# Four head pairs of the third batch transposed by DMA, the loads behind them held, and two edits in the first batch

## The chip, the cores and the metric

The kernel runs on one core of one Trainium2 chip. A core has TensorE (PE, with its weight loads as PEld), VectorE (DVE), ScalarE (ACT), GpSimd (POOL) and SyncE (SP), and 16 DMA engines that all queues share. The metric is the device time of one execution in microseconds; lower is better. Before the change three runs took 434.40 to 435.32 us, with a median of 434.78.

## The reference

There are 8 batches of 12 heads, with 448 positions and a head width of 64. Attention comes without a softmax, and behind it a gated feed-forward layer with 1536 inner columns:

```python
scores = scale * q @ k.T                # per batch and head, scale = 1/8
attn   = maximum(scores, 0) ** 2 / 448
x      = (attn @ v), heads side by side # 3584 x 768
out    = (maximum(x @ w_gate, 0) * (x @ w_val)) @ w_out
```

Inputs and output are float32. The kernel works in bfloat16 with float32 sums.

## The kernel before

All matmuls go through `mm` (L64). The heads are taken in six pairs per batch, and two pairs make a quad. For a score matmul both keys and queries must lie with the head width on the partitions, while they are loaded with positions on the partitions (`load_nat`, L109, two DMAs on POOL's queue: one for 64 partitions with four positions each, one for 64 partitions with three; the queue also turns float32 into bfloat16). So each pair has to be transposed, and there are two ways:

- On PE (batches 0, 1 and 2): `transposes` (L168) makes 16 small PE transposes into a PSUM tile `kq_ps`, and one DVE copy (L179) of 960 columns brings keys and queries to SBUF as `kq_sb`. 64 of the copied columns, between keys and queries, are not used.
- By DMA (batches 3 to 7, `PE_B = 3`): `dma_transposes` (L146) regroups all heads of the batch with one DVE copy for keys and one for queries (L151, into `kr` and `qr`), and SP issues four DMA transposes for each (L154), into `kT` and `qT`. The fourth of four has 64 rows, the others 128. There is one `kr` and one `qr`; `kT` and `qT` exist twice, by even and odd batches. `operands` (L157) gives the scores the one or the other.

**Order of the work.** Each engine runs its instructions in program order; the order is written out by hand. `batch(b)` (L436) takes 24 tiles in eight steps of three: six score tiles of pairs, a shared last tile and one "av" entry per quad (`tiles_later`, L351). A score tile goes through ACT's relu (L184) and DVE's square (L188) to `attn`; the values of a quad are cast by DVE (L458) to `xT`. Step n = 2 holds the last tile of the first quad, its "av", and the first score tile of pair 2. Between the steps stand "gaps", in which the feed-forward units of the batch before are run: twelve gate-and-value units (`gv_unit`, L257: twelve gate matmuls, ACT's relu L265, twelve value matmuls, DVE's product L271), then output units (`out_unit`, L283), whose results ACT copies (L294) and SP writes out (L302) from three `o_sb` buffers. `PAIRS_AT` (L434) says after which step which pair is transposed: pairs 2, 3, 4 and 5 in steps 0, 1, 3 and 4, and pairs 0 and 1 of the next batch in step 7. These transposes are put in `midway`, which runs between a unit's gate and value matmuls, or in the middle of an output unit. In the batches from b = 2 on, `dma_transposes(b + 1)` is called in step n = 2.

**Loads.** Keys, queries and values of batch b + 1 are issued in step 0 of batch b, all on POOL's queue. POOL runs ahead of the other engines: an issue waits only until its buffer (two per tensor, by even and odd batches) is free, or until the eighth DMA before it on this queue has landed. At the start (L333 to L344) the first four heads' keys come by SP and ACT; POOL loads queries 0 to 3, keys 4 to 7, queries 4 to 7, keys 8 to 11, queries 8 to 11, then values, the gate and value weights in four pieces, batch 1, and `load_wo` (the output weights in two halves).

**The first batch** (`first_batch`, L378) has no units to fill PE. It runs 21 score tiles, with `idle_matmuls` between them, and ends with six value computations in PSUM (`values`, `av_pair`), which `cast` brings to `xT`: four on DVE (L392) and two on ACT (L390). The names `u2`, `w0` and `w1` are score tiles; `relu2` issues a tile's relu on ACT and its square on DVE.

Of the kernel before, what the change touches and what calls it, by code (L numbers as in the profile page):

```python
# [10 lines left out]
BF16 = mybir.dt.bfloat16  # L11
# [5 lines left out]
def kernel(  # L17
# [15 lines left out]
    nc = tc.nc  # L33

    B, H, S, D = q.shape
    d_model, d_ff = moe_w_gate.shape
# [3 lines left out]
    HP = H // 2  # L40
# [9 lines left out]
    const = ctx.enter_context(tc.tile_pool(name="const", bufs=1))  # L50
    xpool = ctx.enter_context(tc.tile_pool(name="xpool", bufs=2))
    kqpool = ctx.enter_context(tc.tile_pool(name="kqpool", bufs=3))
# [7 lines left out]
    def pin(ins):  # L60
        return tc.keep_in_program_order(ins)
# [10 lines left out]
    NB = 2  # L72
# [4 lines left out]
    kn_b = [const.tile([128, H, 4, D], BF16, name=f"kn{i}") for i in range(NB)]  # L77
    qn_b = [const.tile([128, H, 4, D], BF16, name=f"qn{i}") for i in range(NB)]
# [11 lines left out]
    def make_ident():  # L90
        pin(nc.gpsimd.affine_select(out=ident, in_=ident, compare_op=ALU.not_equal, fill=1.0, base=0,  # L91
                                    pattern=[[-1, 128]], channel_multiplier=1))

    def dma_in(o, i):
        pin(nc.gpsimd.dma_start(out=o, in_=i))  # L95
# [13 lines left out]
    def load_nat(dst, src, b, h0, h1):  # L109
        lo = src[b, h0:h1, 0:256, :].rearrange("h (j i) d -> j h i d", i=4)  # L110
        hi = src[b, h0:h1, 256:448, :].rearrange("h (j i) d -> j h i d", i=3)
        dma_in(dst[0:64, h0:h1, :, :], lo)
        dma_in(dst[64:128, h0:h1, 0:3, :], hi)

    def load_qk(b, h0=0, h1=H):
        load_nat(kn_b[b % NB], k, b, h0, h1)
        load_nat(qn_b[b % NB], q, b, h0, h1)

    def load_v(b):
        load_nat(v_b[b % NB], v, b, 0, H)  # L120
# [19 lines left out]
            dma_in(wo_sb[c], rows.rearrange("(kf p) m -> p kf m", p=128))  # L140


    PE_B = 3
    kT_b = [const.tile([128, HP, 512], BF16, name=f"kT{i}") for i in range(NB)]
    qT_b = [const.tile([128, HP, 512], BF16, name=f"qT{i}") for i in range(NB)]
    def dma_transposes(b):  # L146

        n = b % NB
        for nat, grp, tr in ((kn_b[n], kr, kT_b[n]), (qn_b[n], qr, qT_b[n])):
            o = grp.rearrange("p i (h d) -> p i h d", d=D)  # L150
            pin(nc.vector.tensor_copy(o, nat.rearrange("p h i d -> p i h d")))  # L151
            for i in range(4):
                r = 128 if i < 3 else 64
                pin(nc.sync.dma_start_transpose(out=tr[:, :, i * 128:i * 128 + r], in_=grp[0:r, i, :]))  # L154


    def operands(b, hp, bank=None):  # L157

        if b >= PE_B:
            n = b % NB  # L160
            return kT_b[n][:, hp, 0:S], qT_b[n][:, hp, 0:S]
        kq = transposes(b, hp, bank)
        return kq[:, 0:S], kq[:, 512:512 + S]

    def sc_tile():
        return psum.tile([128, 2, 512], FP32, name="sc_ps", tag="sc", bufs=3)
# [1 line left out]
    def transposes(b, hp, bank):  # L168
        if bank is None:
            ps = psum.tile([128, 2048], BF16, name="kq_ps", tag="sc", bufs=3)  # L170
        else:
            ps = bank.bitcast(BF16)
        for t, c0 in ((kn_b[b % NB], 0), (qn_b[b % NB], 512)):
            for i in range(4):
                for h2 in range(2):
                    o = ps[h2 * 64:h2 * 64 + 64, c0 + i * 128:c0 + i * 128 + 128]
                    pin(nc.tensor.transpose(o, t[:, 2 * hp + h2, i, :], ident))  # L177
        kq = kqpool.tile([128, 512 + S], BF16, name="kq_sb")
        pin(nc.vector.tensor_copy(kq, ps[:, 0:512 + S]))  # L179
        return kq  # L180

    def relu_part(src, n):
        r = rpool.tile([128, 2, S], BF16, name="r_sb")[:, :n, :]
        pin(nc.scalar.activation(r, src, AF.Relu))  # L184
        return r

    def square_part(dst, r):
        pin(nc.vector.tensor_tensor(dst, r, r, ALU.mult))  # L188

    def relu2(src, dst, n):  # L190
        square_part(dst, relu_part(src, n))
# [40 lines left out]
    def bank_tile():  # L232
        return psum.tile([128, 512], FP32, name="xT_ps", tag="acc", bufs=2)
# [18 lines left out]
    def flush():  # L252
        flush_relu()
        while late_squares:
            square_part(*late_squares.pop(0))
# [69 lines left out]
    def gap():  # L325

        n, of, i = share
        for _ in range((i + 1) * n // of - i * n // of):
            ffn.pop(0)()
        flush()  # L330
        share[2] = i + 1

    load_first(4)  # L333
    make_ident()
    load_qk(0, 4, 8)
    load_qk(0, 8, H)
    load_v(0)
    load_gv(0)
    load_gv(1)
# [22 lines left out]
    def burst(b, tiles):  # L362

        todo, begun = [], None
        for qd, kind, c, i in tiles:
            attn = attn_of(b, qd)
            if kind == "pair":
                todo.append(scores(kqs[b, 2 * qd + c], i, attn, 8 * c + 2 * i))
            elif kind == "last":
                todo.append(scores_last((kqs[b, 2 * qd], kqs[b, 2 * qd + 1]), attn))  # L370
            else:
                ps = sc_tile()
                banks = [ps[:, c, :S] for c in range(2)]
                av_last(b, qd, attn, banks)
                begun = (qd, banks, ps[:, :, :S])
        return todo, begun

    def first_batch():  # L378

        def tile_of(n, i):  # L380
            return burst(0, [tiles_first[3 * n + i]])[0][0]

        def values(qd, c):
            ps, x = bank_tile(), xT_of[0][:, 2 * qd + c, :]
            av_pair(0, qd, c, attn_of(0, qd), ps)
            return x, ps[:, :S]

        def cast(x, ps, on_act=False):
            if on_act:
                pin(nc.scalar.activation(x, ps, AF.Copy))  # L390
            else:
                pin(nc.vector.tensor_copy(x, ps))  # L392

        bank = bank_tile()
        idle_matmuls(bank, 14)
        transpose_pair(0, 0, bank)
        bank = bank_tile()
        idle_matmuls(bank, 4)
        for n in range(5):
            t = [tile_of(n, i) for i in range(3)]  # L400
            if n == 4:
                low_values(0)
            transpose_pair(0, n + 1, bank)
            if n < 4:
                bank = bank_tile()
                idle_matmuls(bank, 2)
                for u in t:
                    relu2(*u)
        relu2(*t[0])
        relu2(*t[1])  # L410
        u0 = tile_of(5, 0)
        cast(*values(0, 0))
        relu2(*t[2])
        u1 = tile_of(5, 1)
        cast(*values(0, 1))
        u2 = tile_of(5, 2)
        relu2(*u0)
        relu2(*u1)
        w0 = tile_of(6, 0)
        cast(*values(1, 0), on_act=True)  # L420
        relu2(*u2)
        w1 = tile_of(6, 1)
        cast(*values(1, 1))
        w2 = tile_of(6, 2)
        relu2(*w0)
        relu2(*w1)
        x, ps = values(2, 0)
        relu2(*w2)
        cast(x, ps, on_act=True)
        cast(*values(2, 1))  # L430
# [5 lines left out]
    def batch(b):  # L436

        gaps = [(1, 1)] * 8
        if b == 1:
            gaps = [(0, 1), (0, 1), (0, 1), (0, 1), (0, 1), (0, 1), (1, 1), (1, 1)]  # L440
        elif b == 2:
            gaps[5] = (0, 2)
        start_gaps(sum(map(sum, gaps)))
        for n in range(len(tiles_later) // 3):
            todo, begun = burst(b, tiles_later[3 * n:3 * n + 3])
            relu2(*todo[0])
            relu2(*todo[1])
            late.extend(todo[2:])
            if n == 1:
                low_values(b)  # L450
            if n == 0 and b < B - 1:
                load_qk(b + 1)
                load_v(b + 1)

            def values():
                qd, banks, both = begun
                av_rest(b, qd, attn_of(b, qd), banks)
                pin(nc.vector.tensor_copy(xT_of[b][:, 2 * qd:2 * qd + 2, :], both))  # L458

            for _ in range(gaps[n][0]):  # L460
                gap()
            for hp in PAIRS_AT.get(n, ()):
                if hp < HP:
                    midway.append(lambda hp=hp: transpose_pair(b, hp))
                elif b + 1 < B:
                    midway.append(lambda hp=hp: transpose_pair(b + 1, hp - HP))
            if begun and (b, n) == (1, 2):
                midway.append(values)
            elif begun:
                values()  # L470
            if b + 1 < B and n == 2 and b + 1 >= PE_B:
                dma_transposes(b + 1)
            for _ in range(gaps[n][1]):
                gap()

    for b in range(B):
        xT_of[b] = xpool.tile([128, KD, S], BF16, name="xT")
# [46 lines left out]
```

## Time and profile before

| | |
|---|---|
| median of three runs | 434.78 us |
| the profiled execution | 435.1 us |
| its span, first to last instruction | 433.3 us |
| PE busy | 425.4 us |
| DVE, ACT busy | 210.7 us, 218.0 us |
| POOL busy | 49.0 us |
| granted PE clock | 1.0 throughout |
| moved by DMA | 42.45 MB |

In the profile each line of a timeline gives the start and the length in us, the engine, the line of the kernel, the operation, output and inputs, their shapes and the count; in brackets stands the idle time of the engine ahead of it and what ended it. "SPq" marks an instruction of SP's queue, such as a DMA issue: its length is that of the issue, and "to landing" counts from the issue's start until the data has arrived. A DMA share over 1 means that packets overlap on the engines. Lengths of matmuls on PE overlap by the pipeline, so what a stretch costs PE is read from the distance between starts.

### The profile page before, as it was taken

To read this page: it belongs to the slowest core of one execution; us is meant where nothing else is said; L and a number is where in the kernel's file an instruction comes from. 1 tells how busy PE (TensorE), PEld (TensorE's weight loads), DVE (VectorE), ACT (ScalarE), POOL (GpSimd) and SP (SyncE) were. 2 spreads that over 40 slices of the span, in tenths; PEclk is the share of its full clock that TensorE was granted. 3 is DMA by queue.
4 is the path that set the end of the run, shared out by engine and by line. 5 is a ranking of instruction groups with operands and counts; after the bars stand their busy time and mean duration, and the time that the engine had idled before them with its cause. 6 is when DMAs were issued, how large, how long until landed. Compare 5 with 4: busy or idle time off the path is not lost.

```text
span 433.3 us, 11436 instructions
## 1 busy us (share of the span) xinstructions
PE 425.4 (98%) x5068; PEld 250.3 (58%) x5068; DVE 210.7 (49%) x334; ACT 218.0 (50%) x325; POOL 49.0 (11%) x71
## 2 busy tenths in 40 slices
PE   8899999999999999999999999999999999999996
PEld 4457655655565555655566555655566555566564
DVE  5952784556623655356532565435643454422210
ACT  4942666454554564465454645554545645532221
POOL 8424311100204000300004000010000000000001
PEclk9999999999999999999999999999999999999999
DMA  9999999905679770591517932170414100030014
GB/s 151 181 205 195 203 205 211 204 5 81 106 145 166 103 112 19 104 198 34 97 38 128 176 66 65 38 138 2 101 29 106 42 2 2 12 100 2 2 38 109
DMA packets 78513, 42.45 MB, mean 98 GB/s; under 512 B 48352, under 2 KB 74976, under 8 KB 78464
## 3 DMA queue, kind: packets, MB, share of 16 engines
q0 software_dynamic: 45120, 23.47, 40.6%
q1 hardware_dynamic: 32992, 18.01, 17.8%
q8 instruction: 39, 0.64, 0.6%
q10 hardware_dynamic: 352, 0.25, 0.2%
q14 instruction: 10, 0.08, 0.1%
HBM read 47.19 MB, written 11.01 MB: 134 GB/s over the span
## 4 chain that ended last, share of the span: by engine, by line
PE 84%; DMA 12%; POOL 2%; issue 1%; POOLq 0%; ACT 0%
PE o_ps L64 25%; PE g_ps L64 23%; PE v_ps L64 22%; PE sc_ps L64 13%; DMA qn<-in_q_dram 5%; DMA wo<-in_moe_w_out_dram 5%; DMA vn<-in_v_dram 2%; POOL qn L95 1%; PE kq_ps L177 1%; POOL kn L95 1%; POOL vn L95 0%; POOL out_dram L302 0%; POOLq L519 0%; ACT o_sb L294 0%; POOL ident L91 0%
## 5 line engine op out<-in xcount | busy, mean ns | idle before, releaser
L184 ACT ACTIVATE r_sb<-sc_ps 128x896 bf16<-128x896 f32 x168 | 145.1, 927 | 39.4 <-PE sc_ps L64 39.4
L188 DVE TENSOR_TENSOR attn<-r_sb 128x896 bf16<-128x896 bf16 x168 | 103.7, 623 | 92.2 <-ACT r_sb L184 92.1
L64 PE MATMUL g_ps<-xT,wg 128*64 128x448 bf16 x1152 | 126.1, 354 | 0.0
L64 PE MATMUL v_ps<-xT,wv 128*64 128x448 bf16 x1152 | 125.2, 352 | 0.0
L64 PE MATMUL o_ps<-wo,hT 128*64 128x384 bf16 (+1 forms) x1368 | 115.3, 324 | 0.3 <-DMA wo<-in_moe_w_out_dram 0.3
L271 DVE TENSOR_TENSOR hT<-v_ps,g_sb 128x448 bf16<-128x448 f32 x96 | 59.9, 624 | 88.4 <-PE v_ps L64 87.5
L64 PEld LDWEIGHTS <-hT 128*64 128x64 bf16 x1368 | 75.5, 110 | 37.8 <-issue 6.5
L265 ACT ACTIVATE g_sb<-g_ps 128x448 bf16<-128x448 f32 x96 | 52.3, 545 | 88.9 <-PE g_ps L64 88.9
L64 PEld LDWEIGHTS <-wg 128*64 128x64 bf16 x1152 | 63.4, 110 | 49.8 <-issue 13.1
L64 PEld LDWEIGHTS <-wv 128*64 128x64 bf16 x1152 | 66.2, 110 | 41.0
L294 ACT ACTIVATE o_sb<-o_ps 128x384 f32<-128x384 f32 (+1 forms) x57 | 27.9, 489 | 81.4 <-PE o_ps L64 81.4
L64 PE MATMUL sc_ps<-attn,vn 128*64 128x448 bf16 (+1 forms) x336 | 35.1, 354 | 0.0
L95 POOL DMA_DIRECT2D vn<-in_v_dram x16 | 12.1, 768 | 168.5 <-PE sc_ps L64 161.0
L458 DVE CAST xT<-sc_ps 128x896 bf16<-128x896 f32 x21 | 22.9, 1091 | 14.3 <-PE sc_ps L64 14.3
L64 PEld LDWEIGHTS <-vn 128*64 128x64 bf16 (+1 forms) x384 | 18.8, 109 | 16.5 <-issue 5.6
L64 PE MATMUL sc_ps<-qT,kT 64*64 64x448 bf16 x420 | 28.4, 357 | 0.0
L64 PE MATMUL sc_ps<-kq_sb 64*64 64x448 bf16 x252 | 19.0, 360 | 1.9 <-ACT r_sb L184 1.7
L95 POOL DMA_DIRECT2D kn<-in_k_dram x18 | 13.3, 762 | 46.8 <-PE kq_ps L177 45.2
L64 PEld LDWEIGHTS <-kT 64*64 64x64 bf16 x420 | 9.6, 105 | 14.3 <-issue 11.7
L302 POOL DMA_DIRECT2D out_dram<-o_sb x2 | 1.1, 558 | 146.2 <-ACT o_sb L294 146.2
L95 POOL DMA_DIRECT2D qn<-in_q_dram x20 | 14.6, 752 | 9.4 <-DMA vn<-in_v_dram 6.3
L64 PEld LDWEIGHTS <-kq_sb 64*64 64x64 bf16 x252 | 6.5, 105 | 13.3 <-issue 9.9
(32 smaller groups left out, 84.2 us busy)
## 6 DMA issues: line engine op xcount, KB each, us to landing
out_dram<-o_sb SPq DMA_DIRECT2D x54, 192.0 KB, 2.7
vn<-in_v_dram POOLq DMA_DIRECT2D x8, 384.0 KB, 7.7
kn<-in_k_dram POOLq DMA_DIRECT2D x7, 384.0 KB, 9.7
qn<-in_q_dram POOLq DMA_DIRECT2D x7, 384.0 KB, 12.2
vn<-in_v_dram POOLq DMA_DIRECT2D x8, 288.0 KB, 8.7
wo<-in_moe_w_out_dram POOLq DMA_DIRECT2D x2, 1152.0 KB, 20.0
kn<-in_k_dram POOLq DMA_DIRECT2D x7, 288.0 KB, 10.9
qn<-in_q_dram POOLq DMA_DIRECT2D x7, 288.0 KB, 13.0
```

Of the source, the lines that this page charges most:

```text
L64: pin(nc.tensor.matmul(o, lhsT=l, rhs=r, start=start, stop=stop, skip_group_check=True))
L95: pin(nc.gpsimd.dma_start(out=o, in_=i))
L177: pin(nc.tensor.transpose(o, t[:, 2 * hp + h2, i, :], ident))
L184: pin(nc.scalar.activation(r, src, AF.Relu))
L188: pin(nc.vector.tensor_tensor(dst, r, r, ALU.mult))
L265: pin(nc.scalar.activation(g_sb, g_ps, AF.Relu))
L271: pin(nc.vector.tensor_tensor(hT[:, mf, col:col + S], v_ps, g_sb, ALU.mult))
L294: pin(nc.scalar.activation(out=o_sb[:, c0:c1], in_=o_ps, func=AF.Copy, scale=float(out_scale)))
L302: pin(e.dma_start(out=segment_rows(b0, 2 * t + s)[:, m], in_=o_sb[s * 64:s * 64 + 64, m]))
L458: pin(nc.vector.tensor_copy(xT_of[b][:, 2 * qd:2 * qd + 2, :], both))
```

## The change

Four edits:

1. Pairs 2 to 5 of batch 2 are taken by DMA too. `dma_transposes` gets the first head as an argument and handles the heads from there on; for batch 2 it is called with head 4 at the end of step 7 of batch 1. Batch 2's pairs 0 and 1 stay on PE. The call for batch 3 moves from step 2 to step 4 of batch 2.
2. Behind the transposes for batch 2, POOL copies one column of `kT` and one of `qT` into a small tile `flag` that nothing reads. A copy waits until the transpose that writes its column has landed, and the loads of batch 3 stand behind the two copies in POOL's queue.
3. In the first batch ACT's cast of the third values comes after the relu of `u2`, not before it.
4. At the start the keys of heads 4 to 11 are loaded with two DMAs instead of four, ahead of all further queries. `kq_sb` holds 2 x 448 columns instead of 960, and its copy leaves the unused columns out.

```diff
     PE_B = 3
+
+    def by_dma(b, hp):
+        return b >= PE_B or b == PE_B - 1 and hp >= 2
+
...
-    def dma_transposes(b):
+    def dma_transposes(b, h0=0):
 
         n = b % NB
         for nat, grp, tr in ((kn_b[n], kr, kT_b[n]), (qn_b[n], qr, qT_b[n])):
             o = grp.rearrange("p i (h d) -> p i h d", d=D)
-            pin(nc.vector.tensor_copy(o, nat.rearrange("p h i d -> p i h d")))
+            pin(nc.vector.tensor_copy(o[:, :, h0:H, :], nat[:, h0:H].rearrange("p h i d -> p i h d")))
             for i in range(4):
                 r = 128 if i < 3 else 64
-                pin(nc.sync.dma_start_transpose(out=tr[:, :, i * 128:i * 128 + r], in_=grp[0:r, i, :]))
+                pin(nc.sync.dma_start_transpose(out=tr[:, h0 // 2:HP, i * 128:i * 128 + r],
+                                                in_=grp[0:r, i, h0 * D:d_model]))
...
-        if b >= PE_B:
+        if by_dma(b, hp):
             n = b % NB
             return kT_b[n][:, hp, 0:S], qT_b[n][:, hp, 0:S]
         kq = transposes(b, hp, bank)
-        return kq[:, 0:S], kq[:, 512:512 + S]
+        return kq[:, 0, :], kq[:, 1, :]
...
-        kq = kqpool.tile([128, 512 + S], BF16, name="kq_sb")
-        pin(nc.vector.tensor_copy(kq, ps[:, 0:512 + S]))
+        kq = kqpool.tile([128, 2, S], BF16, name="kq_sb")
+        pin(nc.vector.tensor_copy(kq, ps[:, 0:1024].rearrange("p (t c) -> p t c", t=2)[:, :, 0:S]))
...
     load_first(4)
     make_ident()
-    load_qk(0, 4, 8)
-    load_qk(0, 8, H)
+    load_nat(kn_b[0], k, 0, 4, H)
+    load_nat(qn_b[0], q, 0, 4, 8)
+    load_nat(qn_b[0], q, 0, 8, H)
...
         w0 = tile_of(6, 0)
-        cast(*values(1, 0), on_act=True)
+        second = values(1, 0)
         relu2(*u2)
+        cast(*second, on_act=True)
         w1 = tile_of(6, 1)
...
-            if b + 1 < B and n == 2 and b + 1 >= PE_B:
+            if b + 1 < B and n == (4 if b + 1 == PE_B else 2) and b + 1 >= PE_B:
                 dma_transposes(b + 1)
             for _ in range(gaps[n][1]):
                 gap()
+            if n == 7 and b + 2 == PE_B:
+                dma_transposes(b + 1, 4)
+                flag = const.tile([128, 2], BF16, name="flag")
+                for i, t in enumerate((kT_b[(b + 1) % NB], qT_b[(b + 1) % NB])):
+                    pin(nc.gpsimd.tensor_copy(flag[:, i:i + 1], t[:, HP - 1, S - 1:S]))
```

## The prediction

> **What bounds the kernel now.** I read the page's busy times first, then its chain of waits, then the windows by stage.
>
> ```profile
> span 433.3 us, 11436 instructions
> ...
> PE 425.4 (98%) x5068; PEld 250.3 (58%) x5068; DVE 210.7 (49%) x334; ACT 218.0 (50%) x325; POOL 49.0 (11%) x71
> ...
> PE 84%; DMA 12%; POOL 2%; issue 1%; POOLq 0%; ACT 0%
> ```
>
> TensorE (PE) is busy for 98% of the span and 84% of the chain that ended last; VectorE (DVE) and ScalarE (ACT) are at half. The other 16% of the chain lies at the start. The windows view cuts the span into the first batch, the stretch until the output weights are in, and (third row) the third batch, b = 2 (columns: window, its length, busy time and instructions of PE, PEld, DVE, ACT, POOL, granted clock, DMA share, GB/s):
>
> ```profile
> 0.00:27.00 27.00, 23.14 (x280) 10.53 (x282) 20.46 (x40) 19.95 (x25) 16.25 (x27) 1.00 1.17 174
> 27.00:63.60 36.60, 36.34 (x471) 23.94 (x468) 20.05 (x33) 17.59 (x26) 9.47 (x13) 1.00 1.36 201
> 80.00:134.60 54.60, 54.60 (x682) 32.48 (x680) 28.00 (x43) 27.36 (x41) 6.53 (x9) 1.00 0.60 100
> ```
>
> In the third batch PE is busy 54.60 of 54.60 us while DVE and ACT need half of that: PE work taken out there shortens the kernel one for one, unless a new wait appears. The start is different. The chain in order of time (start, length, what), and the PE row at which it leaves the loads:
>
> ```profile
> 8.55 10.05 DMA vn<-in_v_dram
> ...
> 18.88 22.11 DMA qn<-in_q_dram
> ...
> 41.85 21.70 DMA wo<-in_moe_w_out_dram
> ```
> ```profile
> 63.60 1.17 PE L64 MATMUL o_ps<-wo,hT 128*64 128x384 bf16 x12 [0.26 <-DMA wo<-in_moe_w_out_dram]
> ```
>
> The second half of the output weights lands at 41.85 + 21.70 = 63.55 us, and PE has by then waited 0.26 us. So PE's own gain before 63.6 us counts only as far as this load also comes earlier.
>
> **The change part by part.**
>
> *Transposes off PE.* The PE rows around one pair's transposes in the third batch, around a unit that has none, and the first scores of the second quad (pair 2):
>
> ```profile
> 84.17 0.39 PE L177 MATMUL kq_ps<-ident,kn 128*64 128x128 bf16 x8
> ...
> 84.61 1.30 PE L64 MATMUL v_ps<-xT,wv 128*64 128x448 bf16 x12
> ...
> 91.55 1.30 PE L64 MATMUL g_ps<-xT,wg 128*64 128x448 bf16 x12
> 92.68 1.30 PE L64 MATMUL v_ps<-xT,wv 128*64 128x448 bf16 x12
> ...
> 94.31 0.36 PE L64 MATMUL sc_ps<-kq_sb 64*64 64x448 bf16 x4
> ```
>
> A pair's 16 transposes take 84.61 - 84.17 = 0.44 us of PE; the other three pairs stand in the same place between a gate and a value matmul. Four pairs: **-1.8 us**. That nothing else fills the hole is seen at 91.55: without transposes the value matmuls follow the gate matmuls after 1.13 us with no wait on ACT or DVE. Their four copies to SBUF (two take 1.22 us in the next fence) leave DVE too, off the path.
>
> *What takes their place.* After the last gap of batch 1, DVE gathers the heads 4 to 11 of keys and queries, and SP issues eight DMA transposes, behind the two writes of the third output tile. The rows (timelines of DVE and SP, then the group of DVE copies that regroup a whole batch):
>
> ```profile
> 78.73 1.22 DVE L179 COPY kq_sb<-kq_ps 128x960 bf16<-128x960 bf16 x2 [0.33 <-PE kq_ps L177]
> 81.49 0.63 DVE L188 TENSOR_TENSOR attn<-r_sb 128x896 bf16<-128x896 bf16 x1 [1.53 <-ACT r_sb L184]
> ```
> ```profile
> 80.67 1.11 SPq L302 DMA_DIRECT2D out_dram<-o_sb  x2
> ```
> ```profile
> L151 DVE COPY kr<-kn 128x3072 bf16<-128x3072 bf16 x5 | 4.7, 950 | 0.0
> ```
>
> Two thirds of 950 ns is 0.63 us a copy, so the two run from 79.95 to about 81.2, inside the 1.53 us in which DVE waits anyway: cost nothing, and at most 1.3 us of delay to the squares if that cover were gone. SP is free at 80.67 + 1.11 = 81.78, when the first copy is done. The eight transposes must have landed when PE reaches 94.31; two pairs' transposes before that point are gone, so the need is at 94.31 - 0.88 = 93.43 on the same clock. How long do eight narrower ones take? No row shows a width of four pairs. The rows of six (one group of eight at 202.7 us, the first group's last two landings, and its first and fourth transpose, of 128 and of 64 rows):
>
> ```profile
> L154 SPq DMA_TRANSPOSE kT<-kr x4: 1212/1241/1257, 202.7 to 206.7; - x4
> L154 SPq DMA_TRANSPOSE qT<-qr x4: 1237/1273/2191, 208.0 to 212.9; - x4
> ...
> DMA to landing us min/median/max: 2.4/2.5/4.2
> ```
> ```profile
> L154 SPq DMA_TRANSPOSE qT<-qr x2: 1263/1278/1292, 109.1 to 110.4; - x2
> ...
> DMA to landing us min/median/max: 2.6/3.2/3.8
> ```
> ```profile
> 100.23 1.30 SPq L154 DMA_TRANSPOSE kT<-kr  x1
> ```
> ```profile
> 105.11 1.26 SPq L154 DMA_TRANSPOSE kT<-kr  x1
> ```
>
> A group lasts from 202.7 to 212.9 + 2.4 = 215.3, that is 12.6 us; the longest from 100.2 to 110.4 + 3.8 = 114.2, that is 14.0 us. The issue is what paces them, 1.25 us each, and it does not fall with half the rows (1.26 against 1.30). It may be fixed per instruction, or go by the six blocks of 128 columns. Upper end, fixed: landing at 81.78 + 12.6 to 14.0 = 94.4 to 95.8, **a stall of 1.0 to 2.4 us**. Lower end, in proportion: about 12.6 x 4/6 = 8.4, landing at 90.2, no stall. I take a part fixed and a part by blocks, about 1.0 us each, since an instruction with half the data keeps its time only if something else than data sets it: 8 x 1.0 + 0.9 for the one long issue that each group has + 1.5 from the last issue's end to landing (2.4 less about 1.0) = 10.4, landing near 92.2, 1.2 us early: no stall.
>
> A page of the Trainium skill speaks against the step: VectorE: DVE Perf Modes, "The three transpose paths", gives 390 ns for one 128x128 block on TensorE and 1309 ns by DMA, and its "Rules for kernel authors" prefer TensorE where the result may go to PSUM. By that figure a lone block costs as much as six do here, which would be the fixed end; no run here shows a single block. Since the trace has PE as the bound and SP idle, the longer time costs only if it lands late.
>
> *The held loads.* The two tiny GpSimd (POOL) copies wait for the transposes, and behind them in POOL's queue stand the fourth batch's six loads, now issued at about 92.5 us, and the fifth batch's. Who waits: DVE's regrouping for batch 3, moved to the fifth step. Its place (DVE's square just ahead of it), the nearest loads of the same shape on an idle DMA queue, and the first use in batch 3:
>
> ```profile
> 112.27 0.62 DVE L188 TENSOR_TENSOR attn<-r_sb 128x896 bf16<-128x896 bf16 x1
> ```
> ```profile
> 113.69 1.49 POOL L95 DMA_DIRECT2D kn<-in_k_dram  x2 [34.63 <-PE kq_ps L177]
> ```
> ```profile
> L95 POOL DMA_DIRECT2D qn<-in_q_dram x1: 776/776/776, 115.9 to 115.9; - x1
> ...
> DMA to landing us min/median/max: 8.0/8.0/8.0
> ```
> ```profile
> 134.58 0.76 PE L64 MATMUL sc_ps<-qT,kT 64*64 64x448 bf16 x12
> ```
>
> Keys and queries landed (115.9 + 8.0) - 113.7 = 10.2 us after their first issue, so at about 102.7; DVE needs them at about 112.3 - 1.3 (three pairs gone) + 0.6 = 111.6: 9 us spare. The transposes then run from about 112.5 to at most 112.5 + 14.0 = 126.5, against a need at 134.58 - 1.8 = 132.8: 6 us spare. Behind them on SP stand the next output writes, some 4 us late; three output buffers take that. Cost: nothing.
>
> *The relu ahead of ACT's cast.* Timelines of ACT, DVE and PE at the end of the first batch:
>
> ```profile
> 22.36 0.54 ACT L390 ACTIVATE xT<-xT_ps 128x448 bf16<-128x448 f32 x1 [0.74 <-PE xT_ps L64]
> ```
> ```profile
> 23.74 0.63 DVE L188 TENSOR_TENSOR attn<-r_sb 128x896 bf16<-128x896 bf16 x1 [0.46 <-ACT r_sb L184]
> ```
> ```profile
> 26.85 0.38 PE L64 MATMUL xT_ps<-attn,vn 128*64 128x448 bf16 x2 [0.43 <-DVE attn L188]
> ```
>
> ACT idles 0.74 us for the values although the next scores lie ready. With the relu first, DVE's 0.46 us of idle time goes and it then runs without a gap; the last square ends about 0.5 us earlier, and with it PE's last values. PE would be 0.5 us ahead from 27 us on, and 0.26 + 0.5 = 0.76 us ahead of the output weights at 63.6.
>
> *Fewer loads of keys.* Two DMA issues fewer on POOL. Two of the startup's issues, PE's transposes of pair 2, the last key load's landing, and the DMA rates while POOL issues and after:
>
> ```profile
> 3.00 1.25 POOL L95 DMA_DIRECT2D kn<-in_k_dram  x2
> ```
> ```profile
> 10.64 0.41 PE L177 MATMUL xT_ps<-ident,kn 128*64 128x128 bf16 x8
> ```
> ```profile
> L95 POOL DMA_DIRECT2D kn<-in_k_dram x1: 697/697/697, 6.0 to 6.0; - x1
> ...
> DMA to landing us min/median/max: 4.3/4.3/4.3
> ```
> ```profile
> 4.00:14.50 10.50, 9.54 (x142) 4.61 (x139) 6.94 (x13) 6.76 (x9) 10.23 (x15) 1.00 1.36 162
> 30.00:63.50 33.50, 33.34 (x440) 21.71 (x436) 18.94 (x32) 16.94 (x25) 8.99 (x13) 1.00 1.37 201
> ```
>
> The queries of pair 2 now come after all keys; the last key load landed at 6.0 + 4.3 = 10.3 us, so by the same bytes the queries land by then, and PE transposes pair 2 only after 10.6: no cost. All later issues come about 1.2 us sooner. The loads moved 162 GB/s while POOL was issuing and 201 later; 1.2 us less at the lower rate gives 1.2 x (1 - 162/201) = 0.2 us, and at most the 1.2 us itself. Between these I take 0.4, near the lower end since later rows show the DMA share full. PE takes it at the output weights, up to its 0.76: **-0.4 us** (0 to -0.76). The narrower copy of kq (896 for 960 columns) saves some 30 ns each, off the path.
>
> *Sum:* -1.8 - 0.4 = -2.2 us. The profiled execution took 435.1 (span 433.3 and 1.8 around it), 0.3 above the median of 434.78; the difference carried to the median gives **432.6**.
>
> **The rivals.** (1) *Late transposes.* Issue is fixed per instruction, PE waits 1.0 us at the second quad's first scores: 434.78 - 2.2 + 1.0 = 433.6, at the longest group 435.0. For it: the 64-row rows. Against: four blocks are less to describe than six. The rule of the Trainium skill above, that a lone block takes 1309 ns (VectorE: DVE Perf Modes, "The three transpose paths"), would give this case. (2) *Weights no earlier.* The load stream goes by bytes; PE's 0.76 us become a longer wait for them: 434.78 - 1.8 = 433.0. For it: the DMA share is above 1 throughout. (3) *The hole is filled*, PE waits elsewhere for what the transposes covered: 434.6. Against: the unit at 91.55. (4) *The held loads make it slower.* If the flags or the loads take 9 us more than counted, DVE blocks at the regrouping, with all squares and products behind it, and PE stops; beyond 2.2 us of such a wait the kernel is slower than before. Should the loads go at half the counted rate and the flags release at 96, keys and queries land at 116.4, 4.8 us late: 434.78 - 2.2 + 4.8 = 437.4. Against: the DMA share in that batch's window, the third row above, is only 0.60.
>
> **How the numbers follow.** Forecast 0.50 (432.6, from 432.2 to 432.9 by the weights alone), late transposes 0.24, weights no earlier 0.15, hole filled 0.05, held loads 0.06. A measurement of this kernel tells about 0.2% (0.87 us) from no change: under 433.91 is faster, over 435.65 slower. Faster: 0.50 + 0.15 + three quarters of 0.24 = 0.83; slower 0.06; the rest, 0.11, the same. The range takes in all of the forecast, the second rival and most of the first: 432.0 to 434.3.
>
> **What will show it.** Only 14 x 16 PE transposes left, and value matmuls directly behind gate matmuls at four places of batch 2. PE's wait ahead of the first scores on kT in batch 2: none by the forecast, 1 us or more by rival 1; the issue time of a narrow DMA transpose decides it (1.0 against 1.25 us). PE's wait for the output weights: about 0.6 us, with their landing near 63.1; 0.8 at 63.5 by rival 2. DVE's regrouping for batch 3 without a wait for a load. The forecast is wrong if PE shows a wait longer than 0.5 us in batches 2 or 3.

## The result, and the profile after

The changed kernel takes 432.51 us (median of four executions, 432.43 to 433.05) against 435.05 for the kernel before (four, 434.40 to 435.45): a ratio of 0.9946, 95% interval 0.9928 to 0.9963. The forecast was 432.6. The profiled execution, of 433.05 us, is the longest of the four; the others' spans are 430.7 and 430.8 us.

The page of the changed kernel, its span, busy times and chain of what ended last:

```profile
span 431.3 us, 11326 instructions
...
PE 424.2 (98%) x5004; PEld 248.6 (58%) x5004; DVE 208.7 (48%) x332; ACT 218.1 (51%) x325; POOL 48.3 (11%) x71
...
PE 93%; DVE 3%; ACT 1%; issue 1%; SPq 1%; DMA 1%; POOL 0%; POOLq 0%; DVEq 0%
```

PE has 64 instructions fewer, four pairs of 16. DMA's part of the chain went from 12% to 1%: loads no longer set the start, where the chain now runs through PE's idle matmuls, DVE's squares and ACT's relus. The windows view of the first stages and of the third batch (columns as in the prediction):

```profile
27.00:63.60 36.60, 36.60 (x478) 24.27 (x476) 20.11 (x34) 17.83 (x26) 9.28 (x12) 1.00 1.37 201
80.00:134.60 54.60, 54.34 (x632) 31.55 (x630) 26.38 (x41) 28.88 (x43) 12.31 (x18) 1.00 0.96 145
4.00:14.50 10.50, 9.65 (x134) 4.87 (x130) 6.38 (x12) 6.18 (x8) 9.92 (x14) 1.00 1.46 183
```

PE now runs without a gap from 27 to 63.6 us, but has a gap in the third batch, where it had none. Between 4 and 14.5 us the loads moved 183 GB/s, 162 before. Two places of PE's timeline fix where the time went, the first output matmuls on the second half of the output weights and the first scores of batch 3; behind them the loads of the output weights (issues, and us from issue to landing):

```profile
62.92 1.14 PE L64 MATMUL o_ps<-wo,hT 128*64 128x384 bf16 x12
```
```profile
132.54 0.76 PE L64 MATMUL sc_ps<-qT,kT 64*64 64x448 bf16 x12
```
```profile
L95 POOL DMA_DIRECT2D wo<-in_moe_w_out_dram x2: 818/822/827, 36.9 to 39.3; - x2
...
DMA to landing us min/median/max: 18.4/20.0/21.6
```

The first stood at 63.60 and was waiting; it is 0.68 us earlier and waits no more, since the weights land at 39.3 + 21.6 = 60.9 in place of 63.55. The second stood at 134.58; it is 2.04 us earlier, all of the difference of the spans (433.3 to 431.3). So 0.68 us were won at the start, 1.36 between the two places, and nothing behind them.

PE's timeline in the third batch, where a pair's transposes used to stand (82.33) and at the second quad's first scores (93.15):

```profile
82.33 1.30 PE L64 MATMUL g_ps<-xT,wg 128*64 128x448 bf16 x12
83.47 1.30 PE L64 MATMUL v_ps<-xT,wv 128*64 128x448 bf16 x12
...
92.53 0.36 PE L64 MATMUL sc_ps<-attn,vn 64*64 64x448 bf16 x4
93.15 0.38 PE L64 MATMUL sc_ps<-qT,kT 64*64 64x448 bf16 x4 [0.26 <-DMA qT<-qr]
```

The value matmuls start 1.14 us behind the gate matmuls, as in a unit without transposes: the hole is gone, 4 x 0.44 = 1.76 us. At 93.15 the matmuls stand 0.62 us behind the ones ahead of them, where the kernel before has 0.2 (94.31 there): a new wait of 0.4 us, of which the profile puts 0.26 down to the last transpose of the queries. 1.76 - 0.4 = 1.36, the gain found above. The transposes (groups of SP's issues, and landing), POOL's flags with the held loads, and DVE's regrouping for batch 2 and for batch 3:

```profile
L159 SPq DMA_TRANSPOSE kT<-kr x4: 1246/1264/1290, 81.5 to 85.4; - x4
L159 SPq DMA_TRANSPOSE qT<-qr x4: 1212/1256/1267, 86.8 to 90.7; - x4
...
DMA to landing us min/median/max: 2.3/2.4/2.6
```
```profile
87.87 0.19 POOL L487 COPY flag<-kT 128x1 bf16<-128x1 bf16 x1 [37.18 <-DMA kT<-kr]
93.06 0.19 POOL L487 COPY flag<-qT 128x1 bf16<-128x1 bf16 x1 [5.00 <-DMA qT<-qr]
93.55 1.49 POOL L95 DMA_DIRECT2D kn<-in_k_dram  x2 [0.30 <-PE sc_ps L64]
```
```profile
79.11 0.68 DVE L156 COPY kr<-kn 128x2048 bf16<-128x2048 bf16 x1
79.71 0.68 DVE L156 COPY qr<-qn 128x2048 bf16<-128x2048 bf16 x1
```
```profile
111.22 0.95 DVE L156 COPY kr<-kn 128x3072 bf16<-128x3072 bf16 x1
```

A transpose of four blocks is issued in 1.21 to 1.29 us, no less than one of six; the last is issued at 90.7 and lands 2.4 us later, just ahead of the flag's copy at 93.06. The held loads start at 93.55, and DVE's copy at 111.22 has no bracket: it waited for nothing.

### The profile page after: what moved, and what is told of

Read it like the earlier page. It is cut to its first block, busy times and chain, and to the rows that moved or that the text cites. A ratio compares the mean times of both kernels' runs of the same rounds, so it can differ in the third digit from the quotient of the medians.

```text
span 431.3 us, 11326 instructions
## 1 busy us (share of the span) xinstructions
PE 424.2 (98%) x5004; PEld 248.6 (58%) x5004; DVE 208.7 (48%) x332; ACT 218.1 (51%) x325; POOL 48.3 (11%) x71
## 4 chain that ended last, share of the span: by engine, by line
PE 93%; DVE 3%; ACT 1%; issue 1%; SPq 1%; DMA 1%; POOL 0%; POOLq 0%; DVEq 0%
PE o_ps L64 26%; PE g_ps L64 25%; PE v_ps L64 24%; PE sc_ps L64 15%; DVE attn L194 2%; PE xT_ps L64 2%; PE kq_ps L183 1%; ACT r_sb L190 1%; SPq L159 1%; DMA qT<-qr 1%; DVE kq_sb L185 0%; PE xT_ps L183 0%; DVE xT L399 0%; DVE vn L125 0%; POOL out_dram L308 0%
## 5 line engine op out<-in xcount | busy, mean ns | idle before, releaser
L64 PE MATMUL sc_ps<-qT,kT 64*64 64x448 bf16 x476 | 32.1, 357 | 0.3 <-DMA qT<-qr 0.3
L64 PEld LDWEIGHTS <-kT 64*64 64x64 bf16 x476 | 10.9, 105 | 16.5 <-issue 13.7
L64 PE MATMUL sc_ps<-kq_sb 64*64 64x448 bf16 x196 | 15.2, 361 | 1.7 <-ACT r_sb L190 1.6
L95 POOL DMA_DIRECT2D qn<-in_q_dram x20 | 14.5, 748 | 5.6 <-DMA vn<-in_v_dram 2.0
L95 POOL DMA_DIRECT2D kn<-in_k_dram x16 | 12.0, 771 | 1.9 <-DMA wv<-in_moe_w_val_dram 0.9
L64 PEld LDWEIGHTS <-kq_sb 64*64 64x64 bf16 x196 | 5.0, 104 | 11.3 <-issue 8.5
```

The source lines that it names most:

```text
L64: pin(nc.tensor.matmul(o, lhsT=l, rhs=r, start=start, stop=stop, skip_group_check=True))
```

## The experiments

Times are medians with their range, unless a single execution is named; each ratio is to the kernel before, run on the same chip between them, with its 95% interval. The first four take the change apart.

**The transposes alone.**

The kernel before with edits 1 and 2; the cast, the key loads and the width of `kq_sb` stay.

```diff
+            if n == 7 and b + 2 == PE_B:
+                dma_transposes(b + 1, 4)
+                flag = const.tile([128, 2], BF16, name="flag")
...
```


> Only the DMA transposes for four pairs of batch 2 and the hold of batch 3's loads; the first batch as before. My theory: PE saves 4 x 0.45 = 1.8 us and gives 0.4 back at the first scores of pair 2, because a DMA transpose takes 1.25 us to issue whether it is four or six pairs wide; the start is untouched, so the second half of the output weights still lands near 63.5 us and PE still waits some 0.4 us for it. In sum 1.4 us less than before. Rival: the 0.4 us at pair 2 were an accident of one execution, and the gain is the full 1.8 us. Second rival: the start is needed for the gain, and this alone gives under 0.5 us.

Measured 433.48 us (433.26 to 433.98), ratio 0.9970 (0.9960 to 0.9981), 1.35 less than the 434.83 of before. PE's timeline at the output weights and at the first scores on `kT`:

```profile
63.67 0.84 PE L64 MATMUL o_ps<-wo,hT 128*64 128x384 bf16 x8 [0.58 <-DMA wo<-in_moe_w_out_dram]
```
```profile
94.08 0.38 PE L64 MATMUL sc_ps<-qT,kT 64*64 64x448 bf16 x4 [0.42 <-DMA qT<-qr]
```

Without the other edits PE stands at the weights as before (63.67), and the new wait of about 0.4 us is there too. The two edits together give 1.76 less that wait.

**The cast alone, the key loads alone, and both.**

```diff
-        cast(*values(1, 0), on_act=True)
+        second = values(1, 0)
         relu2(*u2)
+        cast(*second, on_act=True)
```
```diff
-    load_qk(0, 4, 8)
-    load_qk(0, 8, H)
+    load_nat(kn_b[0], k, 0, 4, H)
+    load_nat(qn_b[0], q, 0, 4, 8)
+    load_nat(qn_b[0], q, 0, 8, H)
```


> Only the relu of the score tile ahead of ACT's cast in the first batch. My theory: PE is 0.3 to 0.6 us ahead from 27 us on, but the second half of the output weights still lands near 63.5 us, where PE waits that much longer; the time is that of before within 0.1 us. Rival: the load stream does not bind PE there and the time falls by 0.3 to 0.6 us.

> Only the keys of heads 4 to 11 in two DMAs, ahead of the queries. My theory: the loads behind them come early enough to fall in with a full queue, the values land 3.5 us earlier and the output weights near 61 us as in the changed kernel, and PE's wait of 0.4 us for them is gone; the first queries land up to 0.4 us later, which can take that back. Time 0.4 us less to 0.1 us more than before. Rival, the prediction's own count: the output weights only 0.4 to 1.2 us earlier, landing between 62.3 and 63.1 us.

> The two start edits together, without the DMA transposes and with the wide copy of kq. My theory: output weights near 61 us, no wait for them, and PE 0.7 us earlier from there on: 0.7 us less than before, more than the sum of the two alone. Rival: the two are independent and their gains add up.

The cast alone: 434.60 us (433.86 to 435.78), ratio 0.9994 (0.9985 to 1.0002). The loads alone: 434.81 (434.63 to 435.42), 1.0001 (0.9992 to 1.0010). Both: 434.08 (433.82 to 434.49), 0.9984 (0.9975 to 0.9993). Against the 434.83 of before that is -0.2, 0.0 and -0.75 us: together they give more than their sum. PE's first gate matmuls behind the first batch, in the kernel before and with the cast alone:

```profile
27.04 1.33 PE L64 MATMUL g_ps<-xT,wg 128*64 128x448 bf16 x12
```
```profile
26.29 1.33 PE L64 MATMUL g_ps<-xT,wg 128*64 128x448 bf16 x12
```

The cast alone brings PE 0.75 us ahead there, more than the 0.3 to 0.6 that I expected. PE's row at the output weights, with the cast alone, with the loads alone, and with both:

```profile
62.78 1.17 PE L64 MATMUL o_ps<-wo,hT 128*64 128x384 bf16 x12 [0.21 <-DMA wo<-in_moe_w_out_dram]
```
```profile
63.37 1.14 PE L64 MATMUL o_ps<-wo,hT 128*64 128x384 bf16 x12
```
```profile
63.04 1.14 PE L64 MATMUL o_ps<-wo,hT 128*64 128x384 bf16 x12
```

With the cast alone PE arrives early and waits for the weights; with the loads alone the weights are there (they landed at 62.25, not near 61 as I expected) and PE arrives no earlier than its own work allows. Both limits have to move, as the prediction's "up to its 0.76" says. With both, the weights landed at 60.91 as in the changed kernel, so that step needs none of the DMA transposes. That the cast alone, which touches no load, shows them at 62.74 suggests that this landing varies by some 0.8 us between executions.

**No hold on the loads.**

```diff
-                flag = const.tile([128, 2], BF16, name="flag")
-                for i, t in enumerate((kT_b[(b + 1) % NB], qT_b[(b + 1) % NB])):
-                    pin(nc.gpsimd.tensor_copy(flag[:, i:i + 1], t[:, HP - 1, S - 1:S]))
```


> The changed kernel without the two small POOL copies, so that the loads of batch 3 go out as soon as their buffers are free (near 63 us) and run beside the transposes of batch 2. Theory that the hold is needed: output writes and transposes share the DMA engines with the loads, the transposes land some 1 us or more later and PE waits that much longer at pair 2; 433.2 us or more. Rival: the issue sets the pace of the transposes, 1.25 us each against under 0.5 us of data, the loads are in by 85 us anyway, and the time is within 0.2 us of the changed kernel's; the hold is then worth nothing.

Measured 441.43 us (440.46 to 444.14), ratio 1.0159 (1.0137 to 1.0182): 8.9 us above the changed kernel. PE's timeline, SP's transposes, and windows of this kernel:

```profile
99.64 0.59 PE L64 MATMUL sc_ps<-qT,kT 64*64 64x448 bf16 x4 [6.68 <-DMA qT<-qr]
```
```profile
L159 SPq DMA_TRANSPOSE kT<-kr x4: 1246/1314/2809, 81.3 to 86.8; - x4
L159 SPq DMA_TRANSPOSE qT<-qr x4: 1247/1672/2750, 88.2 to 94.4; - x4
...
DMA to landing us min/median/max: 5.1/9.2/10.1
```
```profile
80.00:95.00 15.00, 12.96 (x144) 7.05 (x140) 8.06 (x14) 8.40 (x13) 2.99 (x4) 1.00 1.45 179
95.58:105.82 10.24, 6.18 (x36) 2.92 (x38) 1.25 (x2) 1.46 (x2) 0.00 (x0) 0.50 0.44 54
```

The same window of the changed kernel, 80 to 95 us:

```profile
80.00:95.00 15.00, 14.74 (x165) 8.12 (x162) 8.46 (x15) 9.33 (x14) 1.82 (x4) 1.00 0.40 89
```

The loads that POOL issues just then, without the hold:

```profile
80.79 1.50 POOL L95 DMA_DIRECT2D kn<-in_k_dram  x2 [2.36 <-PE sc_ps L64]
82.26 1.52 POOL L95 DMA_DIRECT2D qn<-in_q_dram  x2
```

These are the keys and queries of batch 4, not of batch 3, whose own went out from 63.2 us on and had landed by 81.3. Batch 4 uses the buffers of batch 2, which are free once DVE has regrouped batch 2 and PE has transposed its pairs 0 and 1; in the kernel before, PE read them until pair 5, and these loads started at 113.69. So the change itself lets them go early, and the hold keeps them, with the values of batch 3 (issued at 76.94), off the transposes.

Beside the loads (DMA share 1.45 for 0.40) a transpose takes 9.2 us to land in place of 2.4, and some issues take twice as long. PE waits 6.68 us. Then comes a second loss, which no theory of mine had: the granted clock is 0.50 until 105.82, so that the 6.18 us after the wait do the work of 3.1. 6.7 + 3.1 less the 0.4 of wait that the changed kernel has too is 9.4; the first scores of the stage behind, at 108.73 for 99.26, stand 9.47 us later. My rival, that the hold is worth nothing, fell.

**One pair for four.** Only pair 5 of batch 2 goes by DMA; the issues then carry one block of 128 columns.

```diff
-        return b >= PE_B or b == PE_B - 1 and hp >= 2
+        return b >= PE_B or b == PE_B - 1 and hp >= 5
...
-                dma_transposes(b + 1, 4)
+                dma_transposes(b + 1, 10)
```


> The changed kernel with only pair 5 of batch 2 by DMA, pairs 2 to 4 back on PE. It is run for the length of one transpose's issue with one block of 128 columns. If the issue is fixed per instruction: 1.2 to 1.25 us each, as with four and six blocks. If it has a part per block: about 0.4 to 0.6 us by the prediction's split. Time about 1.35 us above the changed kernel's less its wait at pair 2: near 433.4.

One execution: 434.0 us, span 432.2, where I expected about 433.4. SP's transposes:

```profile
L159 SPq DMA_TRANSPOSE kT<-kr x4: 1182/1228/1231, 81.3 to 85.0; - x4
L159 SPq DMA_TRANSPOSE qT<-qr x4: 1177/1229/1889, 86.4 to 90.8; - x4
...
DMA to landing us min/median/max: 2.3/2.3/3.9
```

One block, four or six: the issue takes 1.2 to 1.3 us, apart from single longer ones (1.89 us here, 2.19 among the rows of six in the prediction).

**Queries ahead of keys.** A score matmul takes all 448 columns of `qT` but only a block of `kT`, so the last transpose of the keys is needed later than the last one of the queries.

```diff
-        for nat, grp, tr in ((kn_b[n], kr, kT_b[n]), (qn_b[n], qr, qT_b[n])):
+        both = ((kn_b[n], kr, kT_b[n]), (qn_b[n], qr, qT_b[n]))
+        for nat, grp, tr in (both[::-1] if h0 else both):
```


> The changed kernel with the four transposes of the queries issued ahead of those of the keys for batch 2. The first score tile of pair 2 needs all four of the queries, but only the first of the keys, so the wait ends with the fifth transpose and not with the eighth, 3 x 1.3 = 3.9 us sooner. My theory (late transposes cost 0.4 us): PE does not wait there, and the time is 0.3 to 0.5 us below the changed kernel's 432.5. Rival: the next tiles wait for the keys instead, or PE loses the same 0.4 us later; then no difference.

Measured 432.14 us (432.01 to 432.51), ratio 0.9935 (0.9922 to 0.9948). PE's timeline:

```profile
92.16 0.38 PE L64 MATMUL sc_ps<-kq_sb 64*64 64x448 bf16 x4
...
92.56 0.36 PE L64 MATMUL sc_ps<-qT,kT 64*64 64x448 bf16 x4
```

The wait is gone: 0.4 us from the scores ahead, with the values between them, and no bracket. The time is 0.37 below the changed kernel's, the size of the wait, though the two intervals overlap. No other kernel here has a lower median.

**Keys in four loads, still ahead of the queries.**

```diff
-    load_nat(kn_b[0], k, 0, 4, H)
+    load_nat(kn_b[0], k, 0, 4, 8)
+    load_nat(kn_b[0], k, 0, 8, H)
```


> The changed kernel with the keys of heads 4 to 11 ahead of the queries as there, but in four DMAs: the order is changed, the count is that of before. Theory that the count matters: POOL comes to the values 1.1 us later, the values land near 17 to 18.6 us and the output weights between 62.5 and 63.5, where PE waits; 0.3 to 0.6 us above the changed kernel. Rival, that the order matters: values near 15 us, output weights near 61, time as the changed kernel's.

Measured 433.73 us (432.21 to 436.09, eight executions), ratio 0.9972 (0.9953 to 0.9991). PE's row at the output weights, and their loads:

```profile
62.39 1.14 PE L64 MATMUL o_ps<-wo,hT 128*64 128x384 bf16 x12
```
```profile
L95 POOL DMA_DIRECT2D wo<-in_moe_w_out_dram x2: 821/824/827, 37.8 to 39.9; - x2
...
DMA to landing us min/median/max: 18.5/20.3/22.0
```

The weights land at 39.9 + 22.0 = 61.9, between 60.9 and 63.55, and PE doesn't wait in this execution, the fastest of the eight (432.21). With times spread over 4 us this does not separate the order of the loads from their number in the time; that stays open. The rate between 4 and 14.5 us speaks for the number: 166 GB/s here and 162 to 169 in the three other kernels with four key loads, 174 to 187 in the ten kernels with two.

**A fifth pair, one step earlier.** On top of the kernel with queries first.

```diff
-        return b >= PE_B or b == PE_B - 1 and hp >= 2
+        return b >= PE_B or b == PE_B - 1 and hp >= 1
...
-            if n == 7 and b + 2 == PE_B:
-                dma_transposes(b + 1, 4)
+            if n == 6 and b + 2 == PE_B:
+                dma_transposes(b + 1, 2)
```


> Edit: on top of the kernel that transposes the queries first, a fifth pair of the third batch (pair 1) goes by DMA too, and the group of eight transposes is issued one step earlier, at the end of step 6 of batch 1, with the flags. Theory (PE is the bound and a pair's transposes cost it 0.44 us; a transpose costs nothing as long as it lands before PE needs it): 432.14 - 0.45 = 431.7 us, no PE wait at the first scores on kT, landings of the eight by about 83 us (first issue near 72, eight issues of 1.25 us, 2.4 us of landing). Rival (the earlier issue lands too late for pair 1, or runs beside the last loads of batch 2 and is stretched): PE shows a wait of 0.5 us or more ahead of the first scores of pair 1, and the time is 432.2 us or above.

> Edit: the kernel with five pairs, and 12 instead of 14 idle matmuls at the very start. In the traces the idle matmuls run at a pitch of 0.373 us until the granted clock reaches 1.0, which came at 4.6 to 6.9 us from one execution to the next; where it came late, pair 0's transposes started at 6.38 us in place of 5.81. Theory A (PE's idle matmuls are in the way when the clock comes late): two matmuls fewer free up to 0.75 us, so executions with a late clock gain 0.4 to 0.6 us, the median lies 0 to 0.4 us below that of the kernel with five pairs and the spread is narrower. Theory B (the clock rises because of the matmuls, so fewer of them bring it later): the first real work runs at half clock, and the time is 0.2 to 0.6 us above. If both medians agree within 0.1 us, the start is set by the first loads.

Measured with 14 idle matmuls 435.46 us (433.73 to 436.72), ratio 1.0008 (0.9993 to 1.0023); with 12, 436.05 (434.82 to 437.07), 1.0021 (1.0009 to 1.0032). The fifth pair made it worse. PE's timeline and the windows behind its wait with 14, then with 12:

```profile
86.23 0.37 PE L64 MATMUL sc_ps<-qT,kT 64*64 64x448 bf16 x1 [2.07 <-DMA kT<-kr]
```
```profile
86.86:90.27 3.41, 3.41 (x21) 1.60 (x20) 1.53 (x3) 2.38 (x4) 3.41 (x5) 0.50 0.94 141
```
```profile
87.18 0.37 PE L64 MATMUL sc_ps<-qT,kT 64*64 64x448 bf16 x1 [2.63 <-DMA kT<-kr]
```
```profile
87.80:91.20 3.40, 3.40 (x39) 2.04 (x38) 2.29 (x5) 2.79 (x4) 3.40 (x5) 1.00 1.02 152
```

The shared last tile of the first quad needs the last block of keys at about 84.2; it landed at 86.2, since SP had two output writes to issue first and began at 73.9, not at 72 as I had counted. That is my rival of the late landing. In the first profile a half clock of 3.41 us follows (1.7 us lost), in the second none. 2.07 + 1.7 - 0.44 = 3.3: the first scores of the stage behind stand at 101.98 for 98.64. The twelve times of the kernel with 14 lie in two groups of six, 433.73 to 434.81 and 436.11 to 436.72, some 2 us apart; those of the kernel with 12 in two of six, 434.82 to 435.58 and 436.52 to 437.07. The profiled execution with the half clock is of an upper group (436.43), the one without of a lower (435.08). The mean granted clock of each execution parts the groups the same way: 0.994 to 0.996 in all twelve of the upper ones, 0.999 or 1.0 in all twelve of the lower ones, and 3.41 us at half clock out of 434.6 make a mean of 0.996.

**Two idle matmuls fewer at the start of the changed kernel.**

```diff
-        idle_matmuls(bank, 14)
+        idle_matmuls(bank, 12)
```


> Edit: the changed kernel with 12 instead of 14 idle matmuls at the very start, nothing else. Theory A: 432.51 less 0 to 0.4 us, so 432.1 to 432.5, with pair 0's transposes at or before 5.8 us even where the full clock comes after 6 us. Theory B: 432.7 to 433.1, with the full clock later than 7 us in the profile.

Measured 433.00 us (432.65 to 435.88), ratio 0.9960 (0.9949 to 0.9972), which overlaps the changed kernel's. The median is that of theory B, the profile is not: full clock came at 5.93 us, not after 7. Nor is it that of theory A, with pair 0's transposes at 5.94. The start isn't settled by this run.

**Batch 1 by DMA too.** On top of the kernel with queries first, without a hold on the loads there.

```diff
-        return b >= PE_B or b == PE_B - 1 and hp >= 2
+        return b >= PE_B or b in (PE_B - 2, PE_B - 1) and hp >= 2
...
+                    if u == 5:
+                        dma_transposes(1, 4)
```


> Edit: on top of the kernel that transposes the queries first, pairs 2 to 5 of the second batch (b = 1) go by DMA too, issued in the sixth feed-forward unit of batch 0, with no hold on the loads. Theory (what made the change work is that the transposes have the DMA engines to themselves): here they share them with the loads of the output weights and of batch 2, so they land 5 to 9 us after issue in place of 2.5, as in the kernel without flags; PE, though spared 1.8 us of transposes, waits for them or for the output weights, and the time is above 432.14, at 434 to 440 us. Rival (the DMA engines have room, as the chain shows no load after the first batch any more): 432.14 - 1.8 = 430.3 us, without a PE wait over 0.3 us in batch 1.

Measured 447.04 us (446.32 to 448.93), ratio 1.0287 (1.0267 to 1.0307). PE's timeline, SP's, the landing of its eight transposes, and the window of the half clock:

```profile
65.84 0.59 PE L64 MATMUL sc_ps<-qT,kT 64*64 64x448 bf16 x4 [12.98 <-DMA kT<-kr]
```
```profile
48.24 15.53 SPq L160 DMA_TRANSPOSE kT<-kr  x4
```
```profile
DMA to landing us min/median/max: 8.0/13.4/17.5
```
```profile
54.79:71.86 17.07, 6.02 (x34) 2.89 (x36) 1.40 (x2) 1.46 (x2) 0.16 (x1) 0.50 1.30 185
```

Four issues take 15.53 us beside the loads, for 5.2 when SP has the DMA engines alone, and PE waits 12.98 us. The half clock costs another (71.86 - 65.84) / 2 = 3.0, and the pairs save 1.76: 14.2 of the 14.9 us that this kernel lies above the one with queries first. The theory's 434 to 440 us were too low, and without the 3.0 us of the clock they would still be: the transposes took 8.0 to 17.5 us to land, for 5 to 9 expected.

## Why the prediction was right, step by step

1. *Four pairs off PE, -1.8 us.* Right: 1.76, at the places named, and nothing fills the hole.
2. *Narrow transposes, "about 1.0 us each", landing near 92.2, no stall.* **This step failed.** The issue is fixed per instruction, 1.2 us for one block as for four and six; my argument that half the data keeps its time "only if something else than data sets it" had the answer in it and was weighed the wrong way. That was rival 1's premise. Its price of 1.0 us was too high all the same: no issue of the group was a long one, and SP began at 81.5, so the last landed at 93.0 rather than 94.4. PE, ahead by its gain at the start, stood ready at 92.7 and not at 93.43, and lost 0.4 us. VectorE: DVE Perf Modes of the Trainium skill, "The three transpose paths", gave 1309 ns for a lone block by DMA; the rows of one block, with medians of 1228 and 1229 ns an issue, agree with it within 7% if it counts the issue, as the prediction took it; from issue to landing a block took 2.3 us (median). The rule would have given the better premise here.
3. *The held loads cost nothing.* Right: the flags ran at 87.87 and 93.06, the loads from 93.55, and neither DVE's regrouping at 111.22 nor PE at 132.54 waits. What the prediction did not see is what the hold is for. Its rival 4 priced loads that come too late; without the hold the transposes come too late, which cost 8.9 us.
4. *Regrouping on DVE hidden.* Right: 0.68 us a copy for 0.63, with 0.40 us of idle time left before DVE's next square.
5. *The relu first, PE up to 0.76 us ahead at the output weights.* The mechanism was right, both sizes were too small. The relu brings PE 0.75 us ahead at 27 us, not 0.5 (the cast alone). The wait for the weights cost 0.44 us, not the 0.26 of the bracket: PE took 36.56 us from its first gate matmuls (27.04) to 63.60, and 36.12 from 26.80 to 62.92 in the changed kernel. In its profiled execution PE was only 0.24 us ahead at 27 us, since its start was 0.57 us later (below); 0.24 + 0.44 are the 0.68.
6. *Fewer key loads, -0.4.* The mechanism was right, the term mis-sized: the weights landed 2.6 us earlier, not 0.4 to 1.2. The stream ran at 183 GB/s for 162 while POOL issued, which by my estimate gives 1.1 us of it (21 GB/s over 10.5 us are 0.22 MB, at 201 GB/s); with the key loads alone the step was 1.3 us. The rest is not explained, and some of it may be variation. So the cap, PE's own lead, set the gain: -0.68 in place of -0.4.
7. *Sum -2.2.* In the profiled executions -1.76 + 0.4 - 0.68 = -2.0, which is what the spans show. A missed wait and a gain taken too small nearly cancel, so the closeness of 432.6 to 432.51 is in part luck. The condition named for a wrong forecast, a PE wait over 0.5 us in batches 2 or 3, did not come, by 0.1 us. That the median fell by 2.5 and the profiled span by 2.0 I put down to the start (below); this is argued, not shown. It fits that the profiled execution with the keys in four loads, whose first transposes start at 5.84 and not at 6.38, reaches the output weights at 62.39 for 62.92.

## What to carry to other kernels

Moving transposes from a busy PE to DMA pays PE's time in full as long as they land before their use, and that is decided by the number of instructions (1.2 us of issue each in these runs, for one block as for six) and by what else the DMA engines move: hold the loads that run beside them, those too that the change itself lets go early, and issue first the operand that the first matmul needs whole. Two edits that each measure as nothing may each lift one of two limits that end together; try them together before dropping them. A wait of a few us on PE can cost half as much again through its clock (6.7 us and 3.1 more, without the hold).

## What was not expected of the hardware

- *The clock after a wait.* A PE wait of 6.68 us brought a granted clock of 0.50 for 10.24 us, one of 12.98 us such a clock for 17.07, one of 2.07 for 3.41, and one of 2.63 none: the lengths are 3, 5 and 1 times 3.41 us. TensorE: Matmul & The Clock Gate of the Trainium skill, "Why this matters for your kernels", asks to avoid idle gaps over about 3 us; the long waits agree, but the one of 2.07 us shows that a shorter gap can be enough. Where the wait falls seems to count. The trace's record of the granted clock opens with full clock at 6.83, 7.00, 4.94 and 7.11 us in these four executions (in the order above), and the half clocks begin 26, 14 and 24 times 3.41 us later, as on a fixed grid. On this grid the wait of 2.07 us lies within one stretch of 3.41 us; the one of 2.63 us is split into 1.07 and 1.56 over two; and the stretches ahead of the two long half clocks hold 2.6 and 1.9 us of wait. So half clock began after a stretch with 1.9 us or more of wait, and not after one with 1.56. Four executions fit this and do not prove it.
- *The clock at the start.* The first idle matmuls have a pitch of 0.37 us; the one of full clock, 0.19, came at 4.6 us in the profiled execution of before and at 6.7 in that of after. There the record of the granted clock opens; ahead of it the views print 1.00 for want of a record, and so the table ahead has 1.0 throughout. PE's timelines there, before and after:

```profile
2.65 3.04 PE L64 MATMUL xT_ps<-blank 128*64 128x448 bf16 x20
5.81 0.41 PE L177 MATMUL xT_ps<-ident,kn 128*64 128x128 bf16 x8
```
```profile
2.65 3.95 PE L64 MATMUL xT_ps<-blank 128*64 128x448 bf16 x20
6.38 0.55 PE L183 MATMUL xT_ps<-ident,kn 128*64 128x128 bf16 x8
```

The same 20 matmuls take 0.9 us longer, and the first transposes start 0.57 us later. Over the twelve other profiles the full clock came at 4.9 to 7.1 us, with nothing in the kernels to order it. The profiled execution of the changed kernel is 0.5 us above the median of its four, which this start would explain; it is not shown.
